# Attention with ten V buffers, shared tails of the query weights, sums in place, and moved x loads and ring writes

## Chip, cores and metric

The kernel runs on one core of a Trainium2 chip. The metric is the device time of one execution in microseconds (us). The engines are named as in the profile: PE multiplies matrices, PEld loads its stationary operand, DVE, ACT and POOL do elementwise work, and SP issues nearly all DMAs.

## What is computed

Two independent attention blocks, A and B, with the same shapes. Their results stand side by side in the output.

```python
B, Sq, D = 16, 144, 448          # H = 16 heads, Dh = 256, Sk = 512
q = (x @ wq).reshape(B, Sq, H, Dh), heads ahead of rows
scores = einsum("bhqd,bhkd->bhqk", q, k_cache) * Dh ** -0.5
p = softmax(scores, axis=-1)
o = einsum("bhqk,bhkd->bhqd", p, v_cache)
out = o as (B, Sq, H * Dh) @ wo
```

All inputs are bfloat16. Each (block, batch, head) has its own K and V of 512 x 256.

## The kernel before

**Units.** A unit is one (block, batch, head); there are NT = 512, 256 of A and then 256 of B. The first P0 = 48 units ("natural") take K by plain loads and transpose it on PE; the others take K by DMA transposes, 16 units (a K wave, 4 MB) at a time, into a ring of 32 units. A step i runs, in this order: Q (x times wq) for unit i + 4, S (scores) for unit i + 3, PV and the sum for unit i, then pieces of the output product (wo) for rows that are complete. In the natural part Q and S lead by one step less.

**Q.** D = 448 is cut in chunks of 128 rows, three whole and a tail of 64. The tail of wq lies in partitions 0 to 63 of a fourth chunk of `wq_sb`, with zeros below it; the same chunk of `xt_sb` holds x's tail, below which a transposing load leaves other data. Two batches share a Q in most of the run (`q_pair`), so every other step has eight matmuls of 288 columns and the steps between have none; for even batches these are the even units, for odd batches the odd ones.

**Softmax.** There is no maximum subtracted. ACT takes exp of S into `pt_sb`; POOL adds the four key chunks in two sums (`t_presum`), the second into `p2_sb`; DVE adds the two halves of partitions (`t_halves`) of two neighbouring units into one `ps_sb`; PE multiplies that with a matrix of ones, once for two units (`t_sum`); ACT takes ln and then exp(-ln) of the sum (`t_ln`, `t_recip`); DVE multiplies PV's result with it into `ring` (`t_evac_ot`, the ring write). DVE also reduces the sums to a largest and a smallest value (`t_check`), from which a flag for a general path is made at the end.

**Order of work.** Each engine has its own list of instructions in the order in which the Python loop at the end adds them (`S.add`); an instruction waits by semaphore for what it reads and for the last reader of what it overwrites. Within one engine nothing is passed. A PSUM bank that another engine used last is also waited for.

**Loads.** All but the first wq load are issued by SP, in one order that a planner makes ahead of time. `load_list` gives each load the time of its first use less a margin, the step from which its buffer is free, and a cost: 1.44 for a V group of two units, 2.4 + 0.97 for each unit of a K wave, 1.3 + 0.55 for each batch of an x group. The planner keeps its own clock of PE, and takes next the load that can start first; among those that can start at once the one with the earliest due time, except that a K wave waits for another load only if that one's latest start falls within the wave's cost plus HOLD. A transposing load right behind a K wave is counted 1.4 cheaper. V groups go round NV = 9 slots, x batches round six. Each planned load is issued in the step in which its buffer comes free, so SP may sit at its semaphore with all later loads behind it.

**Lines.** L1132 is Q's matmul, L1145 and L1146 its eviction into `qt_sb`; L1163 S; L1173 exp; L1183 and L1188 POOL's sums; L1197 the halves sum; L1219 PV; L1235 the matmul with ones; L1243 ln; L1256 exp(-ln); L1271 the ring write; L1286 and L1292 the checks; L1335 the output product. DMAs: L1039 K waves, L1053 V, L1068 natural K, L981 to L989 x, L944 and L946 wq, L955 wo, L1364 stores.

## Time and profile before

| What | us |
|---|---|
| median of 12 runs (lowest, highest) | 1049.75 (1046.45, 1053.71) |
| the profiled execution | 1050.05 |
| its span, first to last instruction | 1048.2 |
| PE busy | 1031.9 |
| ACT busy | 794.4 |
| DVE busy | 736.9 |
| POOL busy | 636.5 |
| PE idle until K (once), until V (four times) | 3.3, 2.8 |
| a K wave of B from issue to landing, median | 25.9 |
| a V group of B from issue to landing, median | 7.7 |

The span is that of the one profiled execution, and the rows below it are of the same one. A busy time counts overlapping instructions of an engine once. A busy PE is not PE at its peak, since matmuls are pipelined; the times between the starts of neighbouring matmuls tell more. Idle time counts only on the engine that sets the end.

### The profile page before, as it was taken

Reading aid. Unit: us, or ns where it says so; the run is one execution under the profiler, and the core shown is the slowest. Engines: PE = TensorE matmul, PEld = TensorE weight load, DVE = VectorE, ACT = ScalarE, POOL = GpSimd, SP = SyncE. Lnnn points to the kernel's source line nnn. Section 1 sums busy time; section 2 is a strip of 40 time slices with the busy share of each in tenths; the row PEclk is TensorE's granted clock in tenths of the full one; section 3 lists DMA queues with packets and bytes.
Section 4 is the critical chain, followed back from the end, with each engine's and each line's share of the span. In section 5 each row is a group of like instructions: output and inputs, shape, how many; then the busy total and the mean of one; then the engine's idle time right before and its main releaser. Section 6 shows DMA issues by size and latency. Waiting matters only on the chain.

```text
span 1048.2 us, 32447 instructions
## 1 busy us (share of the span) xinstructions
PE 1031.9 (98%) x12432; PEld 876.3 (84%) x12432; DVE 736.9 (70%) x2042; ACT 794.4 (76%) x2368; POOL 636.5 (61%) x1030
## 2 busy tenths in 40 slices
PE   8999999999999999999999899999999999999997
PEld 8999888888888888888888688888888888888885
DVE  6776677777776766777776577777676676677775
ACT  6877678778777777878767578787877777788785
POOL 3655556666666666666655456666666656666673
PEclk9999999999999999999999999999999999999999
DMA  9999999999999999999999999999999999999970
GB/s 322 362 349 328 291 277 308 279 257 264 308 286 298 296 251 247 280 299 276 291 290 365 256 267 287 282 279 299 276 280 263 269 273 304 273 265 286 291 234 13
DMA packets 590884, 294.10 MB, mean 281 GB/s; under 512 B 501440, under 2 KB 515904, under 8 KB 590720
## 3 DMA queue, kind: packets, MB, share of 16 engines
q1 hardware_dynamic: 590240, 291.72, 111.5%
q8 instruction: 99, 1.62, 0.6%
q14 instruction: 65, 0.53, 0.1%
q10 hardware_dynamic: 480, 0.23, 0.1%
HBM read 161.74 MB, written 4.13 MB: 158 GB/s over the span
## 4 chain that ended last, share of the span: by engine, by line
PE 90%; DMA 5%; ACT 2%; SPq 2%; DVE 1%; issue 0%; POOL 0%; ACTq 0%; DVEq 0%
PE s_ps L1163 23%; PE ot_ps L1219 23%; PE qp_ps L1132 22%; PE op_ps L1335 18%; DMA kt_sb<-in_B_k_cache_dram 2%; DMA v_sb<-in_B_v_cache_dram 2%; PE ot_ps L1235 2%; PE s_ps L1083 1%; PE qp_ps L1083 1%; DMA v_sb<-in_A_k_cache_dram 1%; ACT rinv_sb L1256 1%; PE qp_ps L1335 1%; ACT pt_sb L1173 1%; SPq L1053 0%; SPq L981 0%
## 5 line engine op out<-in xcount | busy, mean ns | idle before, releaser
L1183 POOL TENSOR_TENSOR pp_sb<-pt_sb 128x288 f32<-128x288 bf16 x512 | 384.9, 752 | 316.2 <-ACT pt_sb L1173 302.1
L1173 ACT ACTIVATE pt_sb<-s_ps 128x288 bf16<-128x288 f32 x1024 | 364.4, 408 | 178.4 <-PE s_ps L1163 172.6
L1271 DVE TENSOR_TENSOR ring<-ot_ps,rinv_sb 128x288 bf16<-128x288 f32 (+2 forms) x640 | 241.7, 394 | 155.7 <-ACT rinv_sb L1256 150.7
L1163 PE MATMUL s_ps<-qt_sb,kt_sb 128*128 128x144 bf16 x4096 | 340.1, 226 | 4.8 <-DMA kt_sb<-in_B_k_cache_dram 3.3
L1219 PE MATMUL ot_ps<-pt_sb,v_sb 128*128 128x144 bf16 x4096 | 340.2, 226 | 2.8 <-DMA v_sb<-in_B_v_cache_dram 2.8
L1163 PEld LDWEIGHTS s_ps<-qt_sb,kt_sb 128*128 128x128 bf16 x4096 | 286.9, 98 | 56.7 <-DVE qt_sb L1146 4.9
L1256 ACT ACTIVATE rinv_sb<-ln_sb 64x144 f32<-64x144 f32 x928 | 298.3, 321 | 24.3
L1132 PE MATMUL qp_ps<-xt_sb,wq_sb 128*128 128x288 bf16 (+1 forms) x2368 | 300.5, 270 | 0.8 <-DVE run_sb L1286 0.7
L1335 PE MATMUL op_ps<-wo_sb,ring 128*128 128x448 bf16 x1120 | 285.9, 353 | 0.0
L1219 PEld LDWEIGHTS ot_ps<-pt_sb,v_sb 128*128 128x128 bf16 x4096 | 274.2, 98 | 4.2 <-issue 1.8
L1132 PEld LDWEIGHTS qp_ps<-xt_sb,wq_sb 128*128 128x128 bf16 x2368 | 211.2, 98 | 75.7 <-DVE run_sb L1286 0.8
L1188 POOL TENSOR_TENSOR p_sb<-pp_sb 128x144 f32<-128x144 f32 x464 | 227.4, 490 | 74.1 <-DVE ps_sb L1197 8.8
L1286 DVE TENSOR_REDUCE run_sb<-ot_ps 128x1 bf16<-128x144 f32 x560 | 146.4, 304 | 78.0 <-ACT ln_sb L1243 45.9
L1197 DVE TENSOR_TENSOR ps_sb<-p_sb 64x144 bf16<-64x144 f32 x464 | 155.2, 334 | 46.2 <-POOL p_sb L1188 32.8
L1146 DVE CAST qt_sb<-qp_ps 128x576 bf16<-128x576 f32 x216 | 161.9, 750 | 16.3 <-PE qp_ps L1132 14.1
L1335 PEld LDWEIGHTS op_ps<-wo_sb,ring 128*128 128x128 bf16 x1120 | 94.0, 98 | 20.7 <-issue 0.5
L1243 ACT ACTIVATE ln_sb<-ot_ps 128x144 f32<-128x144 f32 x232 | 67.9, 293 | 34.2 <-PE ot_ps L1235 27.4
L1235 PE MATMUL ot_ps<-ps_sb,ones 128*128 128x144 bf16 x280 | 63.3, 226 | 0.0
L1145 DVE CAST qt_sb<-qp_ps 128x288 bf16<-128x288 f32 x80 | 35.8, 447 | 1.4 <-PE qp_ps L1132 1.1
L1091 ACT ACTIVATE kt_sb<-qp_ps 128x512 bf16<-128x512 bf16 x48 | 28.9, 602 | 1.0 <-PE qp_ps L1083 1.0
L1188 POOL TENSOR_TENSOR ps_sb<-pp_sb 128x144 bf16<-128x144 f32 x48 | 23.5, 489 | 6.9 <-PE ot_ps L1235 0.3
L1235 PEld LDWEIGHTS ot_ps<-ps_sb,ones 128*128 128x128 bf16 x280 | 27.4, 98 | 0.0
(37 smaller groups left out, 162.4 us busy)
## 6 DMA issues: line engine op xcount, KB each, us to landing
v_sb<-in_A_v_cache_dram SPq DMA_DIRECT2D x128, 512.0 KB, 7.1
v_sb<-in_B_v_cache_dram SPq DMA_DIRECT2D x128, 512.0 KB, 7.7
v_sb<-in_A_k_cache_dram SPq DMA_DIRECT2D x22, 512.0 KB, 10.0
out_dram<-ost_sb SPq DMA_DIRECT2D x36, 112.0 KB, 6.1
wo_sb<-in_A_wo_dram SPq DMA_DIRECT2D x8, 448.0 KB, 8.0
wo_sb<-in_B_wo_dram SPq DMA_DIRECT2D x8, 448.0 KB, 8.2
wq_sb<-in_B_wq_dram SPq DMA_DIRECT2D x4, 768.0 KB, 9.5
wq_sb<-in_A_wq_dram SPq DMA_DIRECT2D x3, 768.0 KB, 9.9
```

Of the source, the lines that this page charges most:

```text
L1132: ins = t.matmul(acc, lhsT=wq_sb[:, kc, c0:c0 + 128], rhs=xt_sb[:, kc, xo:xe + 1:max(xe - xo, 1), :], start=(kc == 0), stop=(kc == 3))
L1146: return v.tensor_copy(qt_sb[:, a:b + 1:b - a, :, :], qp_ps[:, :, 0:2 * SQ].rearrange("p e (u q) -> p u e q", u=2))
L1163: ins = t.matmul(s_ps[bank][:, (c % 2) * SQ:(c % 2 + 1) * SQ], lhsT=kt_sb[:, 2 * c + dc, ko:ko + 128], rhs=qt_sb[:, qsl, dc, :], start=(dc ...
L1173: return a.activation(pt_sb[:, psl, 2 * k:2 * k + 2, :].rearrange("p b q -> p (b q)"), s_ps[bank][:, 0:2 * SQ], AF.Exp, scale=DH ** -0.5)
L1183: return g.tensor_tensor(pp_sb[:, :, :], pt_sb[:, psl, 0:2, :], pt_sb[:, psl, 2:4, :], op=ALU.add)
L1188: return g.tensor_tensor(dst, pp_sb[:, 0, :], pp_sb[:, 1, :], op=ALU.add)
L1197: return v.tensor_tensor(ps_sb[p0:p0 + 64, sl, :], p2_sb[0:64, :], p2_sb[64:128, :], op=ALU.add)
L1219: ins = t.matmul(ot_ps[ob][:, dc * SQ:(dc + 1) * SQ], lhsT=v_sb[:, vsl, j, c * DH + dc * 128:c * DH + (dc + 1) * 128], rhs=pt_sb[:, sl, c, ...
L1256: return a.activation(rinv_sb[p0:p0 + 64, sl, :], ln_sb[h0:h0 + 64, :], AF.Exp, scale=-1.0)
L1271: ins = v.tensor_tensor(ring[:, 2 * h:2 * h + 2, r0:r0 + q1 - q0], ot_ps[ob][:, 0:2 * SQ].rearrange("p (c q) -> p c q", c=2)[:, :, q0:q1], ...
L1286: return v.tensor_reduce(run_sb[:, k, j:j + 1], ot_ps[ob][:, 2 * SQ:3 * SQ], axis=AX.X, op=op)
L1335: ins = t.matmul(acc[0:m, 0:D], lhsT=ring[:, c, col0:col0 + m], rhs=wo_sb[:, c, :], start=(c == op_first), stop=(c == op_last))
```

## The change

- V gets ten slots.
- The tails of wq move to `wqt_sb`: the even head of each two in partitions 0 to 63, the odd head in 64 to 127, so that one 128-row weight serves two heads. A load of wq issues two tail DMAs (rows of 512 bytes) in place of one. For even heads x's tail stands in partitions 0 to 63 with zeros below, for odd heads a copy of it (`xu_sb`) stands in 64 to 127 with zeros above. The copy and the zeros are made on DVE, two or three steps ahead of the first Q of a batch (`t_tail_x`).
- POOL's second sum stays in `pp_sb`; `ps_sb` has one slot (in the natural part odd units use half of an output buffer); ln and exp(-ln) share the slots of `rinv_sb`. The checks are gathered 20 at a time and no longer 28.
- x loads count 2.0 + 0.55 for each batch, are due two steps earlier, and follow a K wave at once if their slots are free; a K wave that will have one behind it leaves V more room (`behind`).
- The ring write of unit i - 1 stands in step i, behind Q's eviction and ahead of S; only the last unit's stays in its own step.

```diff
-    NV, NX = 9, 6
+    NV, NX = 10, 6
-    NQT, NPT, NPS, NRI, NOST = 11, 4, 2, 2, 2
+    NQT, NPT, NRI, NOST = 11, 4, 2, 2
-    MARGIN, HOLD, K_FIX = 1.0, 1.0, 2.4
+    MARGIN, HOLD, K_FIX, X_HOLD = 1.0, 1.0, 2.4, 1.0
-    NRUN = max(n for n in range(1, 33) if NCK % n == 0)
+    NRUN = max(n for n in range(1, 21) if NCK % n == 0)
...
-        wq_sb = sb("wq_sb", [128, 4, H * DH], BF16)
+        wq_sb = sb("wq_sb", [128, 3, H * DH], BF16)
+        wqt_sb = sb("wqt_sb", [128, H // 2 * DH], BF16)
+        xu_sb = sb("xu_sb", [128, NX, SQ], BF16)
-        ps_sb = sb("ps_sb", [128, NPS, SQ], BF16)
+        ps_sb = sb("ps_sb", [128, SQ], BF16)
-        p2_sb = sb("p2_sb", [128, SQ], F32)
-        ln_sb = sb("ln_sb", [128, SQ], F32)
...
-                return v.memset(wq_sb[64:128, 3, :], 0.0)
+                return v.memset(xu_sb[0:64, :, :], 0.0)
...
+            p0, p1 = h0 // 2, (h1 + 1) // 2
+            tails = [] if h0 % 2 else [0, 1]
...
-                return q.dma_start(wq_sb[0:64, 3, cols], w[384:448, cols]).then_inc(sems[sem], 16)
+                for k in tails:
+                    src = w[384:448, p0 * 2 * DH:p1 * 2 * DH].rearrange("p (g e n) -> p g e n", e=2, n=DH)[:, :, k, :]
+                    dst = wqt_sb[k * 64:k * 64 + 64, p0 * DH:p1 * DH].rearrange("p (g n) -> p g n", n=DH)
+                    ins = q.dma_start(dst, src).then_inc(sems[sem], 16)
+                return ins
...
+        def t_tail_x(g):
+            sl = g % NX
+
+            def e1(v):
+                return v.tensor_copy(xu_sb[64:128, sl, :], xt_sb[0:64, 3, sl, :])
+            S.add(DVE, e1, reads=[(("xt", sl), g)], writes=[(("xu", sl), g)], name="xu%d" % g)
+            if g in X_AT:
+                return
+
+            def e2(v):
+                return v.memset(xt_sb[64:128, 3, sl, :], 0.0)
+            S.add(DVE, e2, reads=[(("xt", sl), g)], writes=[(("xt", sl), g)], name="xz%d" % g)
...
+                        w, x = wq_sb[:, kc, c0:c0 + 128] if kc < 3 else wqt_sb[:, h // 2 * DH + dc * 128:][:, 0:128], xt_sb[:, kc]
+                        if kc == 3 and h % 2:
+                            x = xu_sb
...
-            dst, key = (ps_sb[:, sl, :], (("ps", sl), U)) if U < P0 else (p2_sb[:, :], ("p2", U))
+            dst, key = ps_natural(U) if U < P0 else (pp_sb[:, 0, :], ("pp", ("p2", U)))
...
-                return v.tensor_tensor(ps_sb[p0:p0 + 64, sl, :], p2_sb[0:64, :], p2_sb[64:128, :], op=ALU.add)
+                return v.tensor_tensor(ps_sb[p0:p0 + 64, :], pp_sb[0:64, 0, :], pp_sb[64:128, 0, :], op=ALU.add)
...
+            if U % 2 == 0:
+                for p0 in (0, 64):
+                    def e(a, p0=p0):
+                        return a.activation(rinv_sb[p0:p0 + 64, 0, :], rinv_sb[0:64, NRI - 1, :], AF.Exp, scale=-1.0)
...
+            def e(a):
+                a.activation(rinv_sb[0:64, NRI - 1, :], rinv_sb[64:128, NRI - 1, :], AF.Exp, scale=-1.0)
+                return a.activation(rinv_sb[64:128, NRI - 1, :], rinv_sb[64:128, NRI - 1, :], AF.Exp, scale=-1.0)
...
-                load(first_q[g0], (g1 - NX) * H - lq(NT) if g1 > NX else s_min, 1.3 + 0.55 * (g1 - g0), t_load_x, XG)
+                load(first_q[g0] - 2, (g1 - NX) * H - lq(NT) if g1 > NX else s_min, 2.0 + 0.55 * (g1 - g0), t_load_x, XG)
...
+            behind = sum(X_HOLD * (m[2] - 1.4) for m in todo[:60] if m[3] is t_load_x and (m[1] == s_min or at(m[1]) + slip <= now))
...
+                if after_k and m[3] is t_load_x and start <= now:
+                    best = (start, latest, m, lo)
+                    break
...
-                        better = best[1] > start + m[2] + HOLD
+                        better = best[1] > start + m[2] + HOLD + behind
                     else:
-                        better = latest <= start + best[2][2] + HOLD
+                        better = latest <= start + best[2][2] + HOLD + behind
...
+            if 0 <= i - 1 < NT - 1:
+                t_evac_ot(i - 1)
             for u in of_step(ls, i):
                 t_s(u)
...
+            for g, at_q in first_q.items():
+                if (-2 + g if g in X_AT else at_q - 2 - g % 2) == i:
+                    t_tail_x(g)
...
-                t_evac_ot(u)
                 if u == NT - 1:
+                    t_evac_ot(u)
                     flag_ev = t_flag()
```

## The prediction

> **What bounds the kernel now.** I read the page's shares first, then the DMA line of its slices, the waits of PE, the DMA queue's timeline, and the matmuls one by one.
>
> ```profile
> PE 1031.9 (98%) x12432; PEld 876.3 (84%) x12432; DVE 736.9 (70%) x2042; ACT 794.4 (76%) x2368; POOL 636.5 (61%) x1030
> DMA  9999999999999999999999999999999999999970
> PE 90%; DMA 5%; ACT 2%; SPq 2%; DVE 1%; issue 0%; POOL 0%; ACTq 0%; DVEq 0%
> ```
>
> PE is never off for long, and the DMA engines are full up to slice 38. Two resources are level; a stage goes to whichever is behind. The waits of PE say where that is DMA:
>
> ```profile
> PE s_ps L1163 <- DMA kt_sb<-in_B_k_cache_dram: 3.3, 1, 3.3
> PE ot_ps L1219 <- DMA v_sb<-in_B_v_cache_dram: 2.8, 4, 1.1
> PE s_ps L1163 <- DVE qt_sb L1146: 0.8, 2, 0.5
> ```
>
> From the start of one matmul to the next it is regularly 63 ns for 144 columns, 123 for 288, 189 for 448. What exceeds that adds up to some 13 us in the whole run: 4.6 in the first 50 us, 3.4 at 598.00 (a K wave that lands late), then 1.3, 0.6, 0.6 and 0.9 at 719.08, 754.00, 814.14 and 881.81 (a V group each), and 0.4 to 0.6 at 433, 497 and 566 (qt). After the K wait the clock drops:
>
> ```profile
> 598.00:602.00 4.00, 4.00 (x25) 2.76 (x26) 0.46 (x1) 1.37 (x4) 1.22 (x2) 0.57 0.98 326
> ```
>
> Columns: window, us, busy and count for PE, PEld, DVE, ACT, POOL, then PEclk, DMA share, GB/s. 0.57 over 4 us costs 1.7 us more. So at most some 8.5 us (0.8%) lie in DMA waits. The queue shows why V is late:
>
> ```profile
> 691.32 22.98 SPq L1039 DMA_TRANSPOSE kt_sb<-in_B_k_cache_dram  x1
> 714.35 3.51 SPq L1053 DMA_DIRECT2D v_sb<-in_B_v_cache_dram  x5
> ```
>
> A K wave holds SP for 23 us; V behind it starts at 714.35, and PE wanted it at 717.8, got it at 719.08.
>
> **The Trainium skill.** "DMA: Bandwidth & Descriptors", section Anatomy of one DMA, says that DMA engines wait on no semaphore; the wait is on the issuing sequencer. The trace agrees: all loads share SP's order, so a load can't pass one that waits for a slot. The same page, section Specifications, gives 512 B as the least transfer at line rate. The new tails have pieces of just 512 B; in the trace's packet records 2,048 B take 92 ns on an engine and 512 B 45 ns, so four small ones cost twice one large one. "TensorE: Matmul & The Clock Gate", section What's actually happening, has half clock after an idle window of about 3.4 us; here a 3.3 us wait brought it, the 1.3 us one did not. "SBUF — State Buffer" calls the port that DVE (with two SBUF inputs) and GpSimd share an exclusive lock; here the halves sum, 0.30 us alone, took 0.52 at 644.85, when POOL was at work.
>
> **The change, part by part.**
>
> *Tenth V slot.* No operation is added. One more group (512 KB, 256 packets of 2,048 B: 256 x 92 / 16 = 1.47 us of DMA) can be ahead where SP waits for a V slot: in A around 262, 330, 360, 390 and 455 us. From 430 to 595 DMA never idles, so a lead earned before is kept up to the K wait at 598: -1.47 there. In B the V loads hardly wait for slots (gaps of 0.04 us between 530 and 840), so there the slot itself gives nothing; order does. Following the planner's rule (V ahead of K if V's latest start is within the K cost plus HOLD), V after the K wave of 691 missed the place ahead by 0.1 us of its due time; the changed costs and slip put it ahead. I take the 1.3 us at 719 as gone. Those at 814 and 882 keep K first; I leave their 1.5 us.
>
> *Shared wq tails.* Matmul count and shapes stay. A four-head load had 64 pieces of 2,048 B (5.9 engine us) and gets 256 of 512 B (11.5): (11.5 - 5.9) / 16 = +0.35 us of DMA, and one more issue on SP, some 0.5 us. The four B loads stand ahead of the late K wave, where DMA is full: +1.41 at 598. In front of the Q wait at 22.87 lies one such load: +0.3. ACT issues one DMA more at the start, hidden by its empty queue.
>
> *Zeros and copies of x.* The 1.77 us memset becomes one of 0.42. 32 copies and 30 memsets of 64 x 144 are new on DVE. Nearest rows: 0.30 (halves sum) and 0.09 (a 64x32 memset): 32 x 0.3 + 30 x 0.1 = 12.6 us. DVE has 311 us free; they stand two steps (4 us) ahead of Q. They wait for the x load, and behind them wait the eviction of qt and so S; the x load's due time moves two steps ahead too, which covers it. Cover gone, a late x costs PE its lateness once per load. Eight more last-level reductions at 0.18: hidden.
>
> *Sums in place.* Today POOL's second sum goes to its own buffer; now it stays in pp_sb, so the next unit's first sum waits for DVE's halves sum, and with one ps_sb an even halves sum waits for the ones-matmul of the pair before. Queued behind it on DVE: the two check reductions, then qt's eviction (S waits for it), then the ring write. One trip, from the rows below: halves 0.30, to POOL 0.09, first sum to second 0.88, second 0.49, to DVE 0.03: 1.79 us.
>
> ```profile
> 642.40 0.30 DVE L1197 TENSOR_TENSOR ps_sb<-p_sb 64x144 bf16<-64x144 f32 x1 [0.30 <-POOL p_sb L1188]
> 643.00 0.52 DVE L1286 TENSOR_REDUCE run_sb<-ot_ps 128x1 bf16<-128x144 f32 x2 [0.29 <-ACT ln_sb L1243]
> 644.08 0.75 DVE L1146 CAST qt_sb<-qp_ps 128x576 bf16<-128x576 f32 x1
> 642.86 0.73 POOL L1183 TENSOR_TENSOR pp_sb<-pt_sb 128x288 f32<-128x288 bf16 x1 [0.49 <-ACT pt_sb L1173]
> 643.74 0.49 POOL L1188 TENSOR_TENSOR p_sb<-pp_sb 128x144 f32<-128x144 f32 x1
> ```
>
> Where Q falls on odd units the other trip goes through DVE's order: halves 0.32, checks 0.44 to 0.6, qt 0.77, ring 0.38 = 1.9 to 2.1. Two units: 3.7 to 3.9 us. PE needs 0.98 + 4 x 0.50 + 0.06 = 3.04 plus four to six wo matmuls (0.19 each): 3.8 to 4.2. It fits with 0 to 0.3 to spare: 0, with a price in the rivals.
>
> *Ring write one step later.* Its stall on ACT (150.7 us of DVE idle before L1271) is gone, so qt is evicted at once. It then ends some 2.4 us into a step with Q, and PV that reuses the bank starts at 2.9: 0.5 spare. The qt waits before 598 are absorbed by the K wait, whose end DMA sets; after it there are only hitches of 0.1 to 0.2, together 0.8: -0.4. ln now waits for the ring write of the unit before (shared rinv slot), 0.35 later at most, with rc and the ring write a step away: 0.
>
> *x behind K.* The planner lets x follow at once. The B load at 745.67 stood behind one V, and V at 749.79 came 0.6 late; it goes directly behind K with one V moved ahead of K: -0.6. The load at 622.56 moves one wave up, behind the K wave of 598: the V after it lands some 4 us later, at 604 to 605, wanted at 607; and the next K wave, with one V ahead, is issued some 3.5 us later and lands at about 629.7, wanted at 631: 0, cover 1.5 us. In A, buffers hide all of it.
>
> Sum: 719 -1.3, 754 -0.6, hitches -0.4, K wait -1.47 + 1.41, start +0.3: about -2.1. The profiled execution took 1050.05 (span 1048.19 and 1.86 around it), so 1047.95; the median is 0.3 below it: 1047.6.
>
> **Unknown costs, both ends.** V waits: -3.4 (all four go) to +1.5 (x behind K makes a new one). K wait: -3.2 (down to 2 us, no half clock) to +2 (tails cost more, no lead). The in-place trip: 0 to +11.6, since a gain is excluded except for POOL and DVE no longer meeting on the port (-0.2 per halves sum, off PE's path). Start: 0 to +1.
>
> **Rivals.**
> 1. The lead pays in full: K wait near 2 us, no clock drop, all V waits gone: -1.5 - 1.7 - 3.4 = -6.6 at the most, 1044 for a typical one. For it: DMA full but for 6 us in each phase. Against it: the tails' 1.41 just ahead.
> 2. It moves waits only: 719 and 754 go, x and the later K wave bring 1.5 to 2 back: 1049.5.
> 3. Slower: the POOL-DVE trip sets the pace. It decides from the point where two units take more than PE's 3.8; each 0.1 above costs 0.1 x 116 pairs (odd-Q batches) = 11.6 us, so 0.04 gives 1054. For it: slack 0 to 0.3. Against: without the meeting on the port the sums run at their short times.
> 4. Slower by DMA: tails and the earlier x push the K wave 3 us later: 1052.5.
>
> The change may also not do what it says: if planner order stays, rival 2.
>
> **How the numbers follow.** Likeliest 0.40 (1046 to 1049), rival 1 0.20, rival 2 0.18, rival 3 0.12, rival 4 0.10. About 0.2% (2.1 us) is what a measurement tells from no change: below 1047.65 is faster, above 1051.85 slower. Half the likeliest and rival 1, with some of rival 2: 0.44 faster; the rest of those 0.34 same; rivals 3 and 4 0.22. Range 1043.5 to 1053.5; signs are mixed, so the likeliest's own stands above.
>
> **What would show it.** Right: PE's wait on V below 1.6 us, no wait at 719 and 754; one K wait of 2.5 to 4 us with PEclk under 1 behind it; DVE idle before the ring write near 0; PE waiting neither on the ring write nor on ps_sb. Wrong: PE waits for ps_sb or qt in odd-Q batches (rival 3); no K wait at all (rival 1); a K wait above 5, or PE behind an x load on DVE (rival 4).

## The result and the profile after

| | before | after |
|---|---|---|
| median, us (runs) | 1049.62 (49) | 1058.03 (12) |
| ratio of the times, 95% interval | | 1.0076 (1.006 to 1.0093) |
| span of the profiled execution, us | 1048.2 | 1060.6 |

The kernel became 8.4 us slower by the medians; the forecast was 1047.6, the range ended at 1053.5. The profiled execution after took 1062.41 us, 4.4 above the median, so its losses add up to more than 8.4. The lines of the page after that answer to those of before, PE's shares, the DMA slices and the chain:

```profile
PE 1036.0 (98%) x12432; PEld 879.4 (83%) x12432; DVE 716.8 (68%) x2112; ACT 794.3 (75%) x2368; POOL 625.3 (59%) x1030
...
DMA  9999999999999999999999999999999999999940
...
PE 88%; DMA 5%; DVE 2%; ACT 2%; POOL 1%; issue 1%; SPq 1%; ACTq 0%; DVEq 0%; POOLq 0%
```

The page hides the cost: the shares are the same to 2%, the DMA row is full as before. The waits of PE (total us, times, longest) tell more:

```profile
PE s_ps L1186 <- DMA kt_sb<-in_B_k_cache_dram: 5.4, 1, 5.4
PE ot_ps L1245 <- DMA v_sb<-in_A_v_cache_dram: 4.0, 1, 4.0
PE ot_ps L1245 <- DMA v_sb<-in_B_v_cache_dram: 3.9, 3, 3.1
```

The V wait in block A is new. It ends at 269.25 us; the K wait ends at 606.51, the longest V wait of B at 887.92. PE's clock falls behind each of the three, in windows of 4 us (columns as in the prediction):

```profile
268.00:272.00 4.00, 2.75 (x21) 2.02 (x22) 0.83 (x3) 0.94 (x3) 1.21 (x2) 0.80 1.04 399
...
608.00:612.00 4.00, 4.00 (x21) 2.37 (x20) 0.02 (x1) 0.71 (x3) 1.22 (x2) 0.53 1.06 253
...
890.00:894.00 4.00, 4.00 (x41) 3.42 (x39) 2.39 (x10) 2.91 (x9) 2.23 (x5) 0.79 1.05 386
```

To place the losses I took from each trace the start of every unit's PV and subtracted the time of the same unit before. For the changed kernel and some experiments of the next section, each in its one profiled execution, in us (b1 has the new load order alone, c1 one moved x load, a1 all but the order, d1 the sums in place alone, b2 the ring write's move alone):

| unit | after | b1 | c1 | a1 | d1 | b2 |
|---|---|---|---|---|---|---|
| 112 (249 us) | 0.16 | 0.47 | 0.23 | 1.68 | 0.11 | 0.35 |
| 128 (281 us) | 5.96 | 2.60 | 4.35 | 3.02 | 1.49 | 0.35 |
| 248 | 5.42 | 2.61 | 4.35 | 2.47 | 1.92 | -0.95 |
| 288 (607 us) | 9.38 | 3.75 | 5.30 | 3.29 | 1.89 | 3.23 |
| 424 | 6.55 | 2.74 | 4.40 | 0.47 | 1.04 | 0.60 |
| 448 (922 us) | 10.90 | 5.83 | 4.13 | -0.46 | 0.46 | -0.32 |
| 504 | 11.96 | 5.81 | 4.12 | 0.56 | 2.10 | -0.84 |

Three steps up in the changed kernel: the V wait of A, the K wait, the V wait of 888. Between 288 and 424 it wins 2.8 back, because V's waits of 719, 754 and 814 us are gone. So are they in a1 and b2, which keep the former load order. What these have in common is a K wait of over 5 us; c1, which comes 5.3 us late from a K wait of 3.2, still waits 1.16 for V at 724.31.

The 1.68 of a1 in the first row is from the start. In the profiles of a1, of a5 and of two experiments further down (p0 and q1, both with the former tails) PE has 38 matmuls between 8 and 12 us, in all others 55 to 62, and is then some 1.9 us late. This comes with and without the change, so it is no part of its cost.

### The profile page after: what moved, and what is told of

Same layout as the page of the kernel before. It is cut to its first block, busy times and chain, and to the rows that moved or that the text cites. A ratio compares the mean times of both kernels' runs of the same rounds, so it can differ in the third digit from the quotient of the medians.

```text
span 1060.6 us, 32420 instructions
## 1 busy us (share of the span) xinstructions
PE 1036.0 (98%) x12432; PEld 879.4 (83%) x12432; DVE 716.8 (68%) x2112; ACT 794.3 (75%) x2368; POOL 625.3 (59%) x1030
## 3 DMA queue, kind: packets, MB, share of 16 engines
HBM read 161.74 MB, written 4.13 MB: 156 GB/s over the span
## 4 chain that ended last, share of the span: by engine, by line
PE 88%; DMA 5%; DVE 2%; ACT 2%; POOL 1%; issue 1%; SPq 1%; ACTq 0%; DVEq 0%; POOLq 0%
PE qp_ps L1155 22%; PE s_ps L1186 22%; PE ot_ps L1245 22%; PE op_ps L1368 18%; DMA kt_sb<-in_B_k_cache_dram 2%; PE ot_ps L1261 1%; DMA v_sb<-in_B_v_cache_dram 1%; PE qp_ps L1103 1%; PE s_ps L1103 1%; POOL pp_sb L1210 1%; ACT pt_sb L1196 1%; DMA wqt_sb<-in_B_wq_dram 1%; PE qp_ps L1368 1%; POOL pp_sb L1215 1%; DMA wqt_sb<-in_A_wq_dram 0%
## 5 line engine op out<-in xcount | busy, mean ns | idle before, releaser
L1210 POOL TENSOR_TENSOR pp_sb<-pt_sb 128x288 f32<-128x288 bf16 x512 | 373.8, 730 | 379.1 <-DVE ps_sb L1223 262.0
L1155 PE MATMUL qp_ps<-xt_sb,wq_sb 128*128 128x288 bf16 (+1 forms) x1776 | 270.1, 271 | 1.8 <-DVE run_sb L1319 0.6
L1304 DVE TENSOR_TENSOR ring<-ot_ps,rinv_sb 128x288 bf16<-128x288 f32 (+2 forms) x640 | 239.2, 390 | 33.5 <-ACT rinv_sb L1283 16.8
L1215 POOL TENSOR_TENSOR pp_sb<-pp_sb 128x144 f32<-128x144 f32 x464 | 227.3, 490 | 36.4
L1223 DVE TENSOR_TENSOR ps_sb<-pp_sb 64x144 bf16<-64x144 f32 x464 | 141.3, 305 | 157.8 <-POOL pp_sb L1215 132.2
L1155 PEld LDWEIGHTS qp_ps<-xt_sb,wq_sb 128*128 128x128 bf16 x1776 | 162.6, 98 | 67.0 <-DVE ps_sb L1223 0.8
L1319 DVE TENSOR_REDUCE run_sb<-ot_ps 128x1 bf16<-128x144 f32 x560 | 145.5, 302 | 28.4 <-ACT rinv_sb L1270 25.2
L1283 ACT ACTIVATE rinv_sb<-rinv_sb 64x144 f32<-64x144 f32 x464 | 149.5, 322 | 13.0
L1270 ACT ACTIVATE rinv_sb<-ot_ps 128x144 f32<-128x144 f32 x280 | 82.6, 295 | 47.6 <-DVE ring L1304 24.9
L1155 PE MATMUL qp_ps<-xu_sb,wqt_sb 128*128 128x288 bf16 (+1 forms) x304 | 81.5, 268 | 0.0
L1288 ACT ACTIVATE rinv_sb<-rinv_sb 64x144 f32<-64x144 f32 x232 | 74.5, 321 | 5.7
L1155 PE MATMUL qp_ps<-xt_sb,wqt_sb 128*128 128x288 bf16 (+1 forms) x288 | 78.8, 274 | 0.0
L1289 ACT ACTIVATE rinv_sb<-rinv_sb 64x144 f32<-64x144 f32 x232 | 74.1, 319 | 2.7
L1261 PE MATMUL ot_ps<-ps_sb,ones 128*128 128x144 bf16 x256 | 58.0, 226 | 0.0
```

The lines of the kernel that those rows point to most:

```text
L1155: ins = t.matmul(acc, lhsT=w, rhs=x[:, xo:xe + 1:max(xe - xo, 1), :], start=(kc == 0), stop=(kc == 3))
L1210: return g.tensor_tensor(pp_sb[:, :, :], pt_sb[:, psl, 0:2, :], pt_sb[:, psl, 2:4, :], op=ALU.add)
L1215: return g.tensor_tensor(dst, pp_sb[:, 0, :], pp_sb[:, 1, :], op=ALU.add)
L1223: return v.tensor_tensor(ps_sb[p0:p0 + 64, :], pp_sb[0:64, 0, :], pp_sb[64:128, 0, :], op=ALU.add)
L1283: return a.activation(rinv_sb[p0:p0 + 64, 0, :], rinv_sb[0:64, NRI - 1, :], AF.Exp, scale=-1.0)
L1304: ins = v.tensor_tensor(ring[:, 2 * h:2 * h + 2, r0:r0 + q1 - q0], ot_ps[ob][:, 0:2 * SQ].rearrange("p (c q) -> p c q", c=2)[:, :, q0:q1], ...
```

## The experiments

Three theories were on the table. O: the new load order holds SP at a slot, V behind it comes late. T: the small packets of the wq tails push K. P: POOL and DVE pass the one sum buffer to and fro. Ratios are to the kernel before, with 95% intervals.

**Order against everything else.** a1 is the changed kernel with the loads in exactly the former order, b1 the kernel before with the new order, a3 the changed kernel with nine V slots, b2 the ring write's move alone.

a1:

```diff
-    NV, NX = 10, 6
+    NV, NX = 9, 6
-                load(first_q[g0] - 2, (g1 - NX) * H - lq(NT) if g1 > NX else s_min, 2.0 + 0.55 * (g1 - g0), t_load_x, XG)
+                load(first_q[g0], (g1 - NX) * H - lq(NT) if g1 > NX else s_min, 1.3 + 0.55 * (g1 - g0), t_load_x, XG)
-                if after_k and m[3] is t_load_x and start <= now:
...
-                        better = best[1] > start + m[2] + HOLD + behind
+                        better = best[1] > start + m[2] + HOLD
...
```

> All of the change but its load order: nine V slots and the former planner rules, which give exactly the former order of loads; shared wq tails, sums in place, ring write one step later stay. Theory O (the new order holds SP and V back): PE's V waits near 269 us (4.15 us and about 1.6 us of half clock) and near 888 us (3.3 us, about 1.5 us of half clock, where the kernel before lost 0.9) go, so 1058.0 - 5.7 - 3.9 = about 1048.5 us. Theory T (the 512-byte tails of wq push the K wave): the K wait near 606 us keeps its 5.6 us and the time stays at 1052 or more. Theory P (POOL and DVE pass the sums to each other in turn): the batch at the end keeps its hitches of 0.3 us and the time stays above 1055.

b1: the same lines the other way round, in the kernel before, still with `NV = 9`.

> The kernel before with the new load order alone (the planner's x rules), nine V slots, former wq tails, sums and ring write. Theory O: the stalls of V near 269 and near 888 us come with the order, and the V waits at 719, 754 and 814 us (2.6 us) go: 1049.6 + 5.7 + 3.9 - 2.6 = about 1056.6 us. Theories T and P: the order is nearly free, 1048 to 1051 us.

a3:

```diff
-    NV, NX = 10, 6
+    NV, NX = 9, 6
```

> The changed kernel with nine V slots in place of ten; its load order differs by one V group alone. If the tenth slot does nothing, the time is the changed kernel's 1058.0 us within 1.5 us; if the slot gives the 1.47 us of lead that the prediction counted, it is some 1.5 us longer and the K wait near 606 us grows from 5.6 to about 7 us.

b2 (before):

```diff
+            if 0 <= i - 1 < NT - 1:
+                t_evac_ot(i - 1)
             for u in of_step(ls, i):
                 t_s(u)
...
-                t_evac_ot(u)
                 if u == NT - 1:
+                    t_evac_ot(u)
```

> The kernel before with the ring write one step later alone. The prediction's step: DVE's idle time before the ring write (155.7 us) falls to some 30 us, PE's waits for qt shrink, and 0.4 us is gained: 1049.2 us. Its rival: the ring write, now ahead of the sum checks and behind qt, makes qt or PV's bank late by turns, and the kernel is 1 to 2 us slower.

| run | median, us | ratio |
|---|---|---|
| a1: all but the order | 1051.29 | 1.003 (1.0016 to 1.0044) |
| b1: the order alone | 1055.79 | 1.0054 (1.0036 to 1.0073) |
| a3: nine slots | 1056.60 | 1.0081 (1.0055 to 1.0108) |
| b2: ring write alone | 1049.95 | 1.0009 (0.9998 to 1.002) |

b1 came out as theory O had it (1056.6), a1 2.8 us above O's 1048.5: two thirds of the loss is the order, about 5.7 us (3.8 to 7.7 by its interval); one third, 2.5 to 3 us, is in the rest. The tenth slot brings no gain that can be seen (a3's 1.0081 against 1.0076; the intervals are too wide to exclude 1.5 us). The ring write's gain of 0.4 us doesn't show in the medians, where a loss of up to 2 us isn't excluded. It does show in the trace where PE no longer waits for DMA: from PV of unit 448 to that of 504 b2 takes 102.60 us, before 103.12, b1 103.10.

The K wait alone was no good witness: PE's waits on K in a1 and in b2, whose loads come in the former order:

```profile
PE s_ps L1186 <- DMA kt_sb<-in_B_k_cache_dram: 4.8, 1, 4.8
```

```profile
PE s_ps L1163 <- DMA kt_sb<-in_B_k_cache_dram: 5.9, 1, 5.9
```

b2 differs from before in nothing that DMA moves, and waits 5.9 where before waited 3.3, so a long K wait is no sign of the new tails. From the issue of the K wave of 491 us to that of the second wave after it (572 before), the six profiles without shared tails (before, b1, b2, and c1, c3, d1 below) took 80.7 to 83.7 us, mean 82.2, the four with them (after, a1, a3, and a5 below) 82.2 to 83.8, mean 83.0.

Over these ten profiles the long K wait goes with the ring write's move. All five with it (b2, a1, a3, a5, after) wait over 5 us for K and not for V between 690 and 820 us; the five without it (before, b1, c1, c3, d1) wait 2.5 to 3.6 us for K and then 1.0 to 2.5 for V. From PV of unit 270 to that of 424 both groups take the same, 308.2 to 311.0 us. K's and V's waits there are one sum. Why the split moves is shown in part: in b2 PE comes to K earlier (262.9 us from unit 112 to 248, before 264.2); the rest is open.

**Parts.** c1 and c3 move one load each in the kernel before, d1 puts the sums in place alone, a5 is a1 with the tenth slot.

c1 (`move(a, b)` puts load a directly behind load b in the finished plan):

```diff
+        move((t_load_x, (1,)), (t_load_k, (2,)))
```

> The kernel before with one load moved: the x load of A that stood six V groups behind a K wave (issued at 145.87 us) now stands directly behind that wave, as in the changed kernel, so that SP waits about 3.5 us for x's slot with V behind it. Theory O (what DMA loses while SP sits at a slot comes back as a V wait and is never made good): V is late near 265 to 270 us, PE loses 2 to 4 us there, the DMA-bound stretch from 490 us on starts as much later, and the time is 1048.8 + 2 to 4 = about 1052 us. Rival (the V groups in the slots cover it; the stall at 269 comes from the other x load, moved ahead of a K wave at 276 us): same time as before.

c3:

```diff
+        move((t_load_v, (213,)), (t_load_k, (25,)))
```

> The kernel before with one V group moved: the last group ahead of the three x loads and the K wave of 859.7 us now stands behind that wave, as in the changed kernel. Theory O: PE's wait near 882 to 888 us grows from 0.9 us to 3 or 4, and half clock follows: 1048.8 + 2 to 4.5 = about 1052 us. Rival (the wait at 888 in the changed kernel came from its late start alone): same as before within 1 us.

d1 (with the single slot of pair sums and the shared slots of ln and exp that go with it):

```diff
-            dst, key = (ps_sb[:, sl, :], (("ps", sl), U)) if U < P0 else (p2_sb[:, :], ("p2", U))
+            dst, key = ps_natural(U) if U < P0 else (pp_sb[:, 0, :], ("pp", ("p2", U)))
...
-                return v.tensor_tensor(ps_sb[p0:p0 + 64, sl, :], p2_sb[0:64, :], p2_sb[64:128, :], op=ALU.add)
+                return v.tensor_tensor(ps_sb[p0:p0 + 64, :], pp_sb[0:64, 0, :], pp_sb[64:128, 0, :], op=ALU.add)
```

> The kernel before with the sums in place alone: POOL's second sum stays in its own buffer, one slot of pair sums, ln and its exp share two slots; former loads, tails and ring write. Theory P (in the last batch PE's load is lightest, and POOL and DVE hand the sum buffer to each other): hitches of 0.3 us appear from about 1020 us on, +1.2 to +1.6 us, 1050.2 us. The prediction's step (the trip of 3.7 to 3.9 us fits beside PE's 3.8 to 4.2): +0, 1048.8 us. If the trip were the pace in all batches: 1054 or more.

a5: as a1, but `NV = 10`.

> The changed kernel with the former planner rules but all ten V slots; its load order is the former one with one V group standing one K wave earlier. Against the same with nine slots (1051.29 us, 1.003 of before): if one more group ahead at 490 us is a lead for the DMA-bound stretch, as the prediction counted, the K wait near 602 us and so the time fall by up to 1.47 us, to about 1049.8 (ratio 1.0016); if the slot gives nothing, the ratio stays at 1.003.

| run | median, us | ratio |
|---|---|---|
| c1: one x load behind K | 1050.96 | 1.0024 (1.0011 to 1.0037) |
| c3: one V group later | 1048.21 | 1.0002 (0.9989 to 1.0015) |
| d1: sums in place | 1051.92 | 1.0025 (1.0013 to 1.0037) |
| a5: a1 with ten slots | 1052.48 | 1.003 (1.0012 to 1.0048) |

O holds for c1 (1052 expected) and falls for c3 (1052 expected); P holds for d1, at twice its price; the slot's 1.47 us did not come. c1 shows the mechanism of O. SP's queue around that load, first before, then c1 (start, us, engine and line, operation, load, count):

```profile
118.35 23.01 SPq L1039 DMA_TRANSPOSE kt_sb<-in_A_k_cache_dram  x1
141.41 2.81 SPq L1053 DMA_DIRECT2D v_sb<-in_A_v_cache_dram  x4
...
144.84 0.98 SPq L1053 DMA_DIRECT2D v_sb<-in_A_v_cache_dram  x2
145.87 7.68 SPq L981 DMA_TRANSPOSE xt_sb<-in_A_x_dram  x1
...
155.47 17.86 SPq L1039 DMA_TRANSPOSE kt_sb<-in_A_k_cache_dram  x1
```

```profile
118.00 23.41 SPq L1039 DMA_TRANSPOSE kt_sb<-in_A_k_cache_dram  x1
145.03 2.31 SPq L981 DMA_TRANSPOSE xt_sb<-in_A_x_dram  x1
...
148.01 4.81 SPq L1053 DMA_DIRECT2D v_sb<-in_A_v_cache_dram  x8
152.87 25.22 SPq L1039 DMA_TRANSPOSE kt_sb<-in_A_k_cache_dram  x1
```

In c1 SP has nothing it may issue from 141.4 to 145.0: x's slot is still being read, and six V groups that before went out in that time stand behind it. The last two columns of the windows (DMA share, GB/s), first before, then c1:

```profile
140.00:145.00 5.00, 5.00 (x63) 4.34 (x62) 3.60 (x11) 3.29 (x10) 2.94 (x5) 1.00 1.13 290
145.00:150.00 5.00, 5.00 (x62) 4.22 (x60) 3.66 (x10) 3.61 (x11) 2.45 (x4) 1.00 1.03 372
```

```profile
140.00:145.00 5.00, 5.00 (x62) 4.31 (x61) 3.60 (x11) 3.41 (x11) 3.00 (x6) 1.00 0.76 174
145.00:150.00 5.00, 5.00 (x63) 4.25 (x61) 3.69 (x9) 3.47 (x11) 2.46 (x5) 1.00 0.78 155
```

116 and 217 GB/s less for 5 us each are 1.7 MB, more than three V groups. The next K wave is issued behind eight V and holds SP for 25.2 us, before 17.9; the backlog is handed on for 120 us, until PE waits 2.5 us for V at 267.62. The clock drop comes on top, and the whole 4.1 us stay to the end (table above). That one execution lost more than the median, 2.6 us.

Nor is the profile before typical: from the second K wave on its V comes earliest of all six with x in its former place. How long before PE's first use the first V group behind each K wave landed, in us, in these six (before, a1, a5, b2, c3, d1) and in the four with x directly behind K (c1, b1, a3, after):

| K wave issued at about | x in its former place | x directly behind K |
|---|---|---|
| 118 us | 8.3 to 9.8 | 2.6 to 4.0 |
| 155 us | 5.2 to 7.9 | 4.0 to 4.8 |
| 180 us | 1.5 to 6.0 | 0.5 to 1.1 |
| 211 us | 1.2 to 4.4 | 0.3 to 0.8 |
| 242 us: PE waits for it | 0 to 1.4 | 2.1 to 4.5 |

The move takes 4 to 7 us of V's lead at once, and the wait that follows is longer in all four. The former order is short of V at the end of this stretch too: c3, a1 and d1 wait 0.4 to 1.4 us there.

d1 shows theory P: its loads are those of before. DVE, POOL and PE's weight load ahead of S in the last batch:

```profile
1023.62 0.30 DVE L1198 TENSOR_TENSOR ps_sb<-pp_sb 64x144 bf16<-64x144 f32 x1 [0.31 <-POOL pp_sb L1190]
...
1025.47 0.30 DVE L1198 TENSOR_TENSOR ps_sb<-pp_sb 64x144 bf16<-64x144 f32 x1 [1.06 <-POOL pp_sb L1190]
...
1026.50 0.44 DVE L1143 CAST qt_sb<-qp_ps 128x288 bf16<-128x288 f32 x1
1027.25 0.30 DVE L1198 TENSOR_TENSOR ps_sb<-pp_sb 64x144 bf16<-64x144 f32 x1 [0.31 <-POOL pp_sb L1190]
```

```profile
1024.07 0.73 POOL L1185 TENSOR_TENSOR pp_sb<-pt_sb 128x288 f32<-128x288 bf16 x1 [0.48 <-DVE ps_sb L1198]
1024.88 0.49 POOL L1190 TENSOR_TENSOR pp_sb<-pp_sb 128x144 f32<-128x144 f32 x1
1025.92 0.73 POOL L1185 TENSOR_TENSOR pp_sb<-pt_sb 128x288 f32<-128x288 bf16 x1 [0.55 <-DVE ps_sb L1198]
```

```profile
1026.99 0.36 PEld L1161 LDWEIGHTS s_ps<-qt_sb,kt_sb 128*128 128x128 bf16 x6 [0.57 <-DVE qt_sb L1143]
```

POOL waits for DVE's halves sum, DVE for POOL's second sum, in a ring: 1023.62 to 1027.25 is 3.63 us for two units. The eviction of qt stands behind the halves sum on DVE, so S and with it PE take the same pace. Before, two units take 3.33 us there (S at 1018.26 and 1021.59). Between matmul starts this appears as eight hitches of 0.3 us from 1008.86 on, 2.4 us, the size of the loss. In the changed kernel the same ring makes POOL wait in the whole run, but PE feels it mostly at the end (seven hitches there):

```profile
L1210 POOL TENSOR_TENSOR pp_sb<-pt_sb 128x288 f32<-128x288 bf16 x512 | 373.8, 730 | 379.1 <-DVE ps_sb L1223 262.0
...
L1304 DVE TENSOR_TENSOR ring<-ot_ps,rinv_sb 128x288 bf16<-128x288 f32 (+2 forms) x640 | 239.2, 390 | 33.5 <-ACT rinv_sb L1283 16.8
```

(The second row is the ring write: its 155.7 us of idle time are down to 33.5, as forecast. What that is worth is seen from unit 448 to 504: a1, a3, a5 and the changed kernel, with the move and the sums in place, take 104.13 to 104.17 us, d1, with the sums in place alone, 104.76.)

**Engines without the pressure of DMA.** p0 to p3 load K and x by plain transfers of the same bytes. K and x then hold their values in another order, so the scores are others; the engines' work is the same.

p0 (before; x likewise, with one plain transfer):

```diff
-                return q.dma_start_transpose(kt_sb[:, :, c0:c0 + n * 128], src).then_inc(sems[sem], 16)
+                return q.dma_start(kt_sb[:, :, c0:c0 + n * 128], src.rearrange("(p n) c -> p (n c)", p=128).rearrange("p (k m) -> p k m", k=8)).then_inc(sems[sem], 16)
```

> The kernel before with every transposing load replaced by a plain load of as many bytes, so that K and x hold their values in another order (the scores are not those of the reference; all instructions of PE, ACT, DVE and POOL stay). DMA has then room to spare. All theories: PE's waits on K and V go (some 11 us with the half clock), the waits of the first 50 us stay: about 1038 us. It is the base for the next three.

p1: p0 with d1's edit.

> The same plain loads with the sums in place. Theory P (POOL's one buffer goes to DVE and back, 3.63 us for two units): the hitches of 0.3 us before S come back in the last batch, eight of them, and with PE never held by DMA perhaps more elsewhere: 2.4 to 4 us above the base. If the 2.5 us of the sums in place came from chance in DMA: as the base within 0.5 us.

p2: p1 with

```diff
+        p2_sb = sb("p2_sb", [128, SQ], F32)
...
-            dst, key = ps_natural(U) if U < P0 else (pp_sb[:, 0, :], ("pp", ("p2", U)))
+            dst, key = ps_natural(U) if U < P0 else (p2_sb[:, :], ("p2", U))
...
-                return v.tensor_tensor(ps_sb[p0:p0 + 64, :], pp_sb[0:64, 0, :], pp_sb[64:128, 0, :], op=ALU.add)
+                return v.tensor_tensor(ps_sb[p0:p0 + 64, :], p2_sb[0:64, :], p2_sb[64:128, :], op=ALU.add)
```

> As the run before it, but POOL's second sum goes to a buffer of its own (576 bytes) as in the kernel before; one slot of pair sums and the shared slots of ln and its exp stay. Theory P: the hitches go, time as the base within 0.5 us. Rival (the single slot of pair sums, or the shared slots, makes the trip): 2.4 us or more above the base, hitches in the last batch.

p3: a1 with p0's and p2's edits.

> With the same plain loads, all of the change but its load order, its tenth V slot and its in-place buffer: shared wq tails, copies and zeros of x on DVE, the ring write one step later, merged slots. If these cost the engines nothing: as the base within 0.5 us; if the ring write's new place or the copies of x hold PE: 1 us or more above, with waits on qt; the small hitches that the ring write was to remove are worth -0.4 us.

The last column is from the one trace: the time from PV of unit 48 to the end, which leaves out the start, the quick and the slow form of it alike.

| run | median, us (lowest, highest) | ratio | from unit 48, us |
|---|---|---|---|
| p0: base | 1042.16 (1041.08, 1042.96) | 0.9926 (0.9907 to 0.9945) | 918.88 |
| p1: sums in place | 1044.31 (1044.05, 1046.14) | 0.9954 (0.9938 to 0.9969) | 921.78 |
| p2: own buffer again | 1043.21 (1042.04, 1043.87) | 0.9939 (0.992 to 0.9959) | 919.91 |
| p3: all but order and buffer | 1043.63 (1043.26, 1044.52) | 0.9943 (0.9924 to 0.9962) | 921.44 |

The base shows what K's and V's lateness is worth in the kernel before: 7 us, not the 11 expected. p1 is 2.15 us above it by the medians, 2.9 from unit 48 on. PE's weight loads waiting for the eviction of a single batch's Q, in p0, p1 and p2:

```profile
PEld s_ps L1152 <- DVE qt_sb L1134: 3.2, 10, 0.7
```

```profile
PEld s_ps L1150 <- DVE qt_sb L1132: 6.0, 10, 0.9
```

```profile
PEld s_ps L1151 <- DVE qt_sb L1133: 3.2, 10, 0.6
```

A buffer of 576 bytes in each partition takes the ring apart: of its eight hitches only the first is left in p2's trace (1000.24 us), and the base has one there too (1001.31). Not all of the cost goes with it. p2 is 1.1 us below p1 and 1.05 above the base by the medians, with intervals that overlap; from unit 48 on it is 1.9 below p1 and 1.0 above the base, in further small waits for qt over the run. The 1.0 belongs to the single slot of pair sums or the shared slots of ln and exp, which p2 keeps; which of the two was not tried.

p3 has no hitches at the end, but ten of 0.3 to 0.5 us over the run before the matmul with ones, whose sum comes late from DVE:

```profile
PEld ot_ps L1251 <- DVE ps_sb L1213: 4.7, 16, 0.5
```

By the medians it is 1.5 us above the base, with overlapping intervals; from unit 48 on 2.6. Which of its edits makes the sum late was not taken apart. The cost doesn't carry over to the changed kernel, which has no such hitches: from PV of unit 290 to that of 424, where nothing of DMA holds it, it takes 259.42 us (a1, a3 and a5 the same within 0.02), p0 259.65, p3 260.89.

**Does the order cost without a full DMA?** q0 to q3 and r0, r1 load x plainly and K in small pieces, as stand-ins for the transposing loads that can be made lighter or heavier. Again the values are in another order. q0 (before):

```diff
-                return q.dma_start_transpose(kt_sb[:, :, c0:c0 + n * 128], src).then_inc(sems[sem], 16)
+                dst = kt_sb[:, :, c0:c0 + n * 128]
+                for k in range(4):
+                    q.dma_start(dst[:, k, :].rearrange("p (n m) -> p n m", m=128),
+                                src[:, k * 128:k * 128 + 128].rearrange("(n p) m -> p n m", p=128)).then_inc(sems[sem], 16)
+                for k in range(4):
+                    ins = q.dma_start(dst[:, 4 + k, :].rearrange("p (r c) -> p r c", c=512),
+                                      src[:, 512:1024].rearrange("(p k r) c -> k p r c", p=128, k=4)[k]).then_inc(sems[sem], 16)
+                return ins
```

> A base for the next three. The kernel before with its transposing loads replaced by plain ones that should fill DMA about as long: of each K wave half goes in pieces of 256 bytes (23 ns each on an engine in the trace of before), half in pieces of 1 KB (51 ns), so 2 MB / 256 B x 23 / 16 = 11.8 us and 2 MB / 1 KB x 51 / 16 = 6.5 us, 18.3 us of DMA for a wave, where the transposing wave took about 17.8 us (4 MB at 235 GB/s). K and x hold their values in another order; all instructions of the engines stay. Expected: DMA as full as in the kernel before and a time near it, 1042 to 1052 us.

q1: b1 with these loads.

> The same loads in the new order (with transposing loads it was 1.0054 of before). If the stand-in for the transposing loads is a fair one: 4 to 7 us above the base, with a V wait near 265 to 270 us. If it lets V pass where the transposing wave did not (SP is held less by it): under 2 us above the base, and then the next two tell little.

q2: q1 with `move((t_load_x, (1,)), (t_load_v, (37,)))`.

> The same loads in the new order but for the x load of A, which goes back to its former place six V groups behind the K wave. With transposing loads its move alone was 1.0024. If the parts add up: some 3 us above the base. If that one move is the whole cost of the order, directly and by what it leaves late: within 1 us of the base.

q3: q0 with five moves in B:

```diff
+        move((t_load_x, (5,)), (t_load_k, (16,)))
+        move((t_load_x, (6,)), (t_load_v, (180,)))
+        move((t_load_v, (182,)), (t_load_x, (6,)))
+        move((t_load_v, (181,)), (t_load_x, (6,)))
+        move((t_load_v, (213,)), (t_load_k, (25,)))
```

> The same loads in the former order but for the moves that lie in B: an x load directly behind the K wave of 600 us, another one K wave earlier, and one V group behind the last x loads. If V's waits at 883 and 911 us in the new order come from these moves: 2 to 3 us above the base. If B's order is free, because there only the sum of bytes counts: within 1 us.

r0: q0 with the first form for all eight chunks (`for k in range(8)`).

> As the base with plain loads whose K waves were half in pieces of 256 bytes, but now all of a K wave goes in pieces of 256 bytes: by the 23 ns of a piece 16384 x 23 / 16 = 23.6 us of DMA for a wave, 5.2 us more than before. From 491 us to the third wave after it the kernel before took 109 us and the lighter base 102.5, of which it waited some 10 us for slots; three waves at 5.2 us more make up for that and a little more. K holds its values in another order; former load order, all instructions of the engines stay. Expected: DMA full without a pause from 490 us on, a K wait near 600 us, time 1046 to 1054 us.

r1: b1 with the loads of r0.

> The same heavier K waves in the new load order. With the lighter waves the new order cost 0 to 1.3 us though SP's wait at x's slot let DMA's share fall to 0.44 at 145 us. Theory O, as it stands now (a pause of DMA costs only where DMA has no room to make it up): 4 to 7 us above the heavier base, with a V wait near 270 us; where further waits lie (before 430 us, or at 883 and 911 us) tells whether the rest of the order's cost comes from A or from the moves in B. If the pause is harmless for another reason than room: within 1.5 us of the base.

| run | median, us (lowest, highest) | ratio | from unit 48, us |
|---|---|---|---|
| q0: base, lighter K waves | 1041.69 (1041.25, 1043.06) | 0.993 (0.9908 to 0.9951) | 918.95 |
| q1: new order | 1043.00 (1041.14, 1043.16) | 0.9933 (0.9912 to 0.9955) | 919.03 |
| q2: new order but one x load | 1041.47 (1040.92, 1043.14) | 0.9926 (0.9905 to 0.9948) | 919.09 |
| q3: moves in B | 1041.44 (1041.31, 1041.98) | 0.9925 (0.9904 to 0.9946) | 918.82 |
| r0: base, heavier K waves | 1065.40 (1064.71, 1071.29) | 1.0179 (1.0152 to 1.0205) | 942.84 |
| r1: new order | 1072.73 (1068.33, 1077.97) | 1.0244 (1.0216 to 1.0271) | 945.78 |

The lighter stand-in missed its aim: there is no K wait, and the time is below the range expected. It shows something else: with room in DMA the order is free. From unit 48 on q0 to q3 agree within 0.3 us, so nothing behind unit 48 makes q1's median 1.3 higher than q0's; its traced execution has the slow start. So q2 and q3 say nothing on which move costs. In q1 SP sits at x's slot as in c1, DMA falls further, and PE doesn't notice:

```profile
145.00:150.00 5.00, 5.00 (x60) 4.24 (x58) 3.56 (x9) 3.22 (x10) 2.44 (x4) 1.00 0.44 135
```

The heavier one missed on the other side (1054 at most was expected). With it DMA is the bound, and the order costs 7.3 us by the medians (some 3 to 11 by the two intervals; r1's times spread over 9.6 us). PE's V waits in r0 and r1:

```profile
PE ot_ps L1212 <- DMA v_sb<-in_B_v_cache_dram: 6.2, 4, 2.5
...
PE ot_ps L1212 <- DMA v_sb<-in_A_v_cache_dram: 4.3, 3, 3.1
```

```profile
PE ot_ps L1212 <- DMA v_sb<-in_B_v_cache_dram: 7.0, 4, 2.6
...
PE ot_ps L1212 <- DMA v_sb<-in_A_v_cache_dram: 5.9, 4, 2.5
```

Those of r1 at 860.07 and 922.68 us (1.95 and 2.77) are not in r0, those of r0 at 734.66 and 830.66 are gone or smaller. So in r1's profile, which lost less than its median, the order costs in A and in B. Here x's slot is free when SP comes (the share at 140 to 150 stays at 0.99 or more), so r1 doesn't repeat c1's stall; what it shares with b1 is the late V in B.

**What stays open.** b1 loses 5.7 us, c1 2.5 of them. b1's profile has the rest in B: V waits of 2.37 us at 883.16 and 1.65 at 911.55. There the new order has 213 V groups ahead of the K wave of 860 (before: 214) and 220 ahead of the next (222). c3 moves the first of these alone and costs nothing, so it is the two together, the earlier x loads, or the late arrival from A; with transposing loads these were not tried apart. a3 has b1's order too, and in B its trace waits only 0.7 us for V, at 910.04; so this part may be larger in b1's one execution than it usually is. Nor were tried, with transposing loads, the new order without c1's move, d1 with its own buffer again, and the whole change without its order and its buffer. No other run with transposing loads is clearly faster than the kernel before.

## Why the prediction was wrong

The step that failed first is a sentence: x behind K, "In A, buffers hide all of it". I priced the other two moved x loads one by one and this one not at all; c1 gives this load alone 2.5 us. (The unknown costs name such a V wait, in general and at 1.5 at most.) In before SP was through with the K wave at 141.4 and came to that load at 145.87. That the slot is read until 144.9 could be looked up (the last Q of its batch); an x load directly behind the wave then waits with V behind it. The changed kernel does, from 141.76 to 145.25. And V is not covered there: 32 of its groups had been issued with PE near unit 57, that is three ahead. At 269.7 us SP waits twice as long for the next x loads, 6.8 us, and nothing more is lost (5.96 at unit 128, 5.42 at 248): nine groups have just been issued, and eight are ahead of PE's. By this one pair the same wait is free or dear by how many V are ahead of PE, and I looked at neither number.

Point by point, by the sum:

- *V waits 719 -1.3 and 754 -0.6*: they went, but not by the order. They went in a1 and b2 too, wherever PE waits over 5 us for K; b1, with the new order and a K wait of 3.2, has in their place 1.6 us of waits for V and K at 695, 758 and 761. V's and K's waits are one sum, and I counted one part as a gain.
- *Tenth slot -1.47*: not found. a5 against a1 and the changed kernel against a3 differ by 0 and 0.0005, but 0.0014 can't be excluded by their intervals.
- *Tails +1.41 at the K wait*: not found either, and mis-sized. The 45 ns for 512 B came from loads of the first 7 us. The 1,024 new packets of B, the only ones of 512 B there, took 29 to 32 ns on average in the four traces that have them. By the prediction's own sum, (256 x 32 - 64 x 92) / 16, that is an estimate of 0.14 us for a load and 0.6 for four. The means of 83.0 and 82.2 agree with it, within a spread of 3 us from run to run. A K wait of 3.3 us in one profile was taken for a property of the kernel.
- *Sums in place 0*: the trip was priced right (3.7 to 3.9 us for two units, measured 3.63), PE's need was not. "3.8 to 4.2" counts 0.98 us for a Q of two batches; the last batch has a single one, 8 matmuls of 144 columns, and before takes 3.33. Rival 3's rule, that each 0.1 us too much costs 0.1 for a pair, is right, with 0.3 us for eight pairs and not for 116: 2.4 us. The term was put at 0 and measured 2.2 (p1) to 2.6 (d1).
- *Ring write -0.4*: right where it can be seen. DVE's idle time went as said; b2 gains 1.3 us before the K wait, which takes it back, as forecast, and 0.5 from unit 448 to 504. The medians, -0.2 to +2 us, can't show it.
- *Zeros and copies of x 0*: nothing in the traces speaks against it; the changed kernel's 259.42 us from unit 290 to 424 are not longer than p0's 259.65.
- Right: the rule that "a load can't pass one that waits for a slot", and the length of the in-place trip. The sign of rival 4 (a K wait above 5) came by luck: b2 has it with the former order and the former tails. Rival 4, slower by DMA, was the nearest, with another mechanism: not more DMA work, but DMA left idle. Rival 3 was right in kind and gave its full price to the wrong stretch.

Measured sum: order 5.7, sums in place 2.6, the rest about 0: 8.3 of 8.4. Each of the two parts is known to 1 or 2 us only, so that they fit this well is luck. Of the order's 5.7, c1 explains 2.5; the cause of the other 3 is open.

## What to carry to other kernels

Before a load is moved ahead in a queue, look up in the trace when its slot comes free and how many loads of the others PE has in hand at that moment: here a wait of 6.8 us cost nothing with eight groups ahead, and one of 3.6 us cost 2.5 us with three. What DMA lost in those 3.6 us was not made up where it was full for the rest of the run (c1), and was where it had room (q1). When a buffer is shared between two engines, compare the round trip with PE's lightest stretch, not with the usual one. When one execution is compared with one, first see whether they start alike.

## What the hardware showed that I had not expected

- When the lower clock comes can be worked out here. The traces record when half the clock was granted. In the ten profiles with transposing loads and those of r0 and r1 there are 17 such stretches between 30 and 1,000 us, of 3.413 us or twice that, and within one run all of them begin and end on one grid of 3.413 us. I took PE's idle time in every window of that grid, with the ends of matmuls as the profile models them. Behind a window at full clock with 2.10 us of it or more half clock followed at once, in all 17 cases; with 1.97 or less never. So the length of a wait alone doesn't decide. c1's V wait of 2.45 us had 2.27 in one window and was followed by half clock; 2.12 us in b1 (267.52), 2.49 in c3 (K, 597.69) and 2.70 in r1 (334.48), which the grid cuts in two, were not. The Trainium skill, "TensorE: Matmul & The Clock Gate", section What's actually happening, speaks of an idle window of about 3.4 us that runs freely; the grid agrees, but by these runs the window need not be idle all through, some 60% of it is enough. Windows of 4 us behind the waits of c1, b1 and c3:

```profile
268.00:272.00 4.00, 4.00 (x31) 3.20 (x29) 2.04 (x5) 1.82 (x6) 0.01 (x1) 0.60 1.05 385
```

```profile
268.00:272.00 4.00, 4.00 (x51) 3.43 (x49) 2.41 (x6) 2.95 (x9) 1.16 (x2) 1.00 1.05 386
```

```profile
600.00:604.00 4.00, 4.00 (x48) 3.28 (x47) 2.54 (x9) 2.84 (x9) 1.95 (x4) 1.00 1.05 396
```

- A transposing K wave of 4 MB holds SP for 16.5 to 26.3 us in the ten profiles with transposing loads, longer the more V groups are still under way: before 16.60 us with none (issued at 859.74), 24.47 with seven (882.67). The wave behind x's slot held it 17.9 to 20.5 us in the six profiles with x in its former place (two V groups under way) and 23.4 to 25.2 in the four with x directly behind K (seven or eight).
- The same loads in the same order took 80.7 us in one profile and 83.7 in another (before and b2, from the K wave issued at 491 us to that at 572).
